# Filler products, a shorter last ranking, an earlier selection matrix and a moved eviction between a delta-rule attention and a sorted mixture of experts

## The chip, the cores and the metric

The kernel runs on one core of a Trainium2 chip. Its time is the device time of one execution in microseconds (us). The core's engines work side by side and wait for each other through semaphores: TensorE (PE, matrix products; its weight loads are listed apart as PEld), VectorE (DVE), ScalarE (ACT), GpSimd (POOL) and SyncE (SP), which here only issues DMA transfers. The profile also shows the share of its full clock that TensorE was granted.

## The reference

An attention block with the delta rule runs over q, k, v of shape (4, 8, 768, 48); its output is read as 3072 tokens of 384 numbers and goes through a mixture of 16 experts (4 groups of 4) of hidden width 1024.

```python
k_n = k / (norm(k) + 1e-6)
for t in range(S):
    y[:, :, t] = q_t @ state
    state = state + beta_t * outer(k_t, v_t - k_t @ state)

x = y.transpose(0, 2, 1, 3).reshape(3072, 384)
g_idx = argmax(x @ w_group);  g_w = softmax(x @ w_group)[g_idx]
e_idx = argmax(x @ w_expert[g_idx]);  e_w = softmax(...)[e_idx]
out = g_w * e_w * (relu(x @ w1[g_idx, e_idx]) @ w2[g_idx, e_idx])
```

Every token goes to one expert.

## The kernel before

**Attention.** The sequence is cut into 24 chunks of 32 steps; one chunk of all four batches fills 128 partitions. Per group of four chunks, `inverse` (L269) inverts the triangular systems on VectorE. The loop over chunks `u` (L675) then does, per chunk: `advance` (L406), whose four steps make a_ps, w_ps, the state update s_bd and the output o_ps, copied to x by ScalarE (L468); and `logits` (L478) for the chunk before, which transposes x (t_ps L485), copies it (xt L489) and multiplies it with the router's weights (l_ps L493, copied to lg L495). x is written to `x_dram` by SP (L733).

**Routing.** `route(r)` (L498) works on a group of chunks: four chunks, and two in each of the last two groups (`groups`, L472). VectorE finds the best group and expert (L516 to L530, `hots` is one-hot), adds up the counts (`acc`, L532), TensorE multiplies with triangular and all-one matrices to rank each token inside its expert (r_ps, L540 and L541), ScalarE copies the ranks (rk, L544) and takes Exp (L545), VectorE makes the rank of each token (`place`, L573), its gate (`what`, third column, L575), the products of `hots` and `what` (`mine`, L577: token's output row, token's input row and gate, for 16 experts) and a one-hot of the place (`at`, L586). TensorE then multiplies `mine` with `at` into s_ps (L593), which ends as a table: for each expert the tokens sent to it. The last group has all of this on the path, since nothing is left to do beside it.

**The order.** In this part it is written by hand: every engine's queue holds its instructions in the order in which the program issues them. `route` and `inverse` are generators; `start` puts them in the list `behind`, `work(n)` lets them issue VectorE work by their share, and `allow(what)` releases those that stopped at a named place (PE_STEP before r_ps, ACT_STEP before the copy of the ranks, SORT before s_ps). After the loop, `while behind` (L736) drains them.

**Handover.** After the loop: n_ps (L745) counts the tokens per expert; `by_place` (L131) turns expert 0's part of s_ps into from_i, to_i and gate; found, last, key, table (L748 to L759) sort the experts by their load. The attention's pools are then closed and those of the experts opened in the same memory. POOL makes a selection matrix `sel` (L926), and gathers the tokens of the first expert from `x_dram` by indirect DMA (`take`, xg, L807), in two tiles of 128 and 96 rows; TensorE transposes them (`turn_in`, t_ps L816), VectorE copies them to xt (L818).

**Experts.** The loop over experts `e` (L951): `hidden` (L846) multiplies xt with w1 in four pairs of column blocks (h_ps L852, 48 records for the 24 products), each pair evicted with Relu by ScalarE (L855); `second` (L865) multiplies with w2 in three thirds of 128 output columns (y_ps L871, two PSUM buffers that take turns), each evicted by ScalarE (yt L873) and followed by `between(j)`, here `late` (L972). At the start of `hidden`, `part_out` (L900) transposes the results of the expert before on VectorE (yq L904), sends them through `y_dram` and reads them back as yr (SP, L908 to L913). `late(0)` transposes the next expert's tokens on VectorE (`cross_in`, xt L832). `late(1)` weighs the results of the expert before with its gates (yo L918, two tiles) and scatters them to the output (POOL, L880). `fetch(e + 2)` issues the gathers of quarter rows for two experts ahead (POOL, xq L824), and after `second` SP issues the weights of expert e + 2 (L164, L171). From expert 1 on the tokens are gathered in quarters, through `quarters` (L836), which uses `sel` (q_ps L841). The last two experts' results leave through TensorE transposes (`turn_out`, L889).

PSUM in the attention part is full: four banks for the state and s_ps, one with tag "s", two with tag "g", one with tag "o" (o_ps).

Of the kernel before, what the change touches and what calls it, by code (L numbers as in the profile page):

```python
# [8 lines left out]
F32 = mybir.dt.float32  # L9
I32 = mybir.dt.int32  # L10
AX = mybir.AxisListType
ALU = mybir.AluOpType
ACT = mybir.ActivationFunctionType
# [53 lines left out]
def deltanet_then_moe(  # L67
# [13 lines left out]
    nc = tc.nc  # L81
# [42 lines left out]
    place = cp.tile([128, NCH], F32, name="place")  # L124
    what = cp.tile([128, NCH, 3], F32, name="what")
    found = cp.tile([128, T, 3, NE], F32, name="found")
    from_i = cp.tile([128, NE, T], I32, name="from_i")
# [47 lines left out]
    with ExitStack() as first:  # L175
# [322 lines left out]
        def route(r):  # L498
# [44 lines left out]
            rk = small("rk", [NE])  # L543
            nc.scalar.activation(rk, r_ps, ACT.Copy)  # L544
            nc.scalar.activation(sx, sx, ACT.Exp)  # L545
# [14 lines left out]
            else:  # L560
                nc.vector.tensor_tensor(rk, rk, hotf, op=ALU.mult)
                yield
# [12 lines left out]
            nc.vector.reciprocal(what[:, u0:u0 + n, 2:3], cw)  # L575
            yield
            (nc.gpsimd if early else nc.vector).tensor_tensor(  # L577
                mine, hotf[:, :, None, :].to_broadcast(like),
                what[:, u0:u0 + n, :, None].to_broadcast(like), op=ALU.mult)
            if early:  # L580
# [57 lines left out]
        with tc.manual_schedule(engines={mybir.EngineType.PE, mybir.EngineType.DVE,  # L638
# [17 lines left out]
            nc.gpsimd.memset(acc[:, 0], 0.0)  # L656
            nc.gpsimd.tensor_copy(what[:, :, 0:2], cut["ids"].rearrange("p (u c) -> p u c", c=2))
            ahead = advance(0)
            next(ahead)
# [13 lines left out]
            allow(FACTOR)  # L673
            ahead_of = {u: [u + LEAD] if u + LEAD < NCH else [] for u in range(NCH + 1)}
            for u in range(NCH + 1):  # L675
                step = advance(u) if u < NCH else iter([None] * 4)
                turned = logits(u - 1) if u else iter([None] * 2)
# [56 lines left out]
                if pieces and u + LEAD >= NCH:  # L734
                    pieces.pop(0)()
            while behind:  # L736
                work(2)
                allow(PE_STEP)
                allow(ACT_STEP)
                allow(SOON)  # L740
                allow(NEXT)
                allow(SORT)

            n_ps = ps.tile([128, NE], F32, tag="s", name="n_ps")
            nc.tensor.matmul(n_ps, lhsT=ones, rhs=acc[:, NCH], start=True, stop=True)  # L745
            by_place(s_sort.rearrange("p (t c e) -> p t c e", t=T, c=3)[:, :, :, 0:FIXED],
                     slice(0, FIXED))
# [116 lines left out]

    def second(hid, yt, w2, between):  # L865

        R = hid.shape[2]
        for j in range(DC):
            y_ps = ps.tile([128, R], F32, tag="y", name="y_ps")
            for f in range(FC):  # L870
                nc.tensor.matmul(y_ps, lhsT=w2[:, f, j * 128:(j + 1) * 128], rhs=hid[:, f],  # L871
                                 start=(f == 0), stop=(f == FC - 1))
            nc.scalar.activation(yt[:, j, 0:R], y_ps, ACT.Copy)  # L873
            between(j)
        return yt
# [45 lines left out]
    def turned():  # L921
        return mp.tile([128, DC, T * TILE], F32, tag="xt", name="xt")

    ready = {e: take(from_i[:, e], tiles_of[e]) for e in range(FIXED)}
    sel = mp.tile([128, 4, 4, BL], F32, name="sel", bufs=1)
    nc.gpsimd.tensor_copy(sel, ident.rearrange("p (g r) -> p g r", r=BL)[:, :, None, :].to_broadcast(  # L926
        [128, 4, 4, BL]))
    xts, yts, rows_of, evs = {0: turned()}, {}, {}, {}
# [15 lines left out]
    with tc.manual_schedule(engines={mybir.EngineType.PE, mybir.EngineType.DVE, mybir.EngineType.SP,  # L944
# [6 lines left out]
        for e in range(NE):  # L951
# [33 lines left out]
            hid = hidden(xts.pop(e), SLOTS[e], w1, early)  # L985
            second(hid, yts[e], w2, late)
            if e + 2 < NE:
# [100 lines left out]
```

## Time and profile before

| what | us |
|---|---|
| median of 4 runs (517.68 to 519.12) | 518.31 |
| the profiled execution's own time | 519.45 |
| its span, first to last instruction | 517.5 |
| TensorE busy, share of the span | 471.2 (91%) |
| attention, with its start, up to the last o_ps | 228.6 |
| last o_ps to the first h_ps (handover) | 15.8 |
| first h_ps to the last product of the last expert | about 264 |
| from there to the span's end | about 9 |

The span is what the profile shows; about 1.95 us of the execution lie outside of it. A page has one digit for each of 40 slices of 12.9 us: busy tenths of each engine and, under PEclk, the clock that TensorE was granted. The chain of waits is followed back from the last instruction: at each place it names what ended the wait. A matmul of fp32 operands is listed as two records. Ends of matmuls are modelled, so a record shows somewhat more than the time its columns take.

### The profile page before, as it was taken

The page shows a single profiled execution, that of the slowest core. Times are in us where ns is not written, and L with a number is a line of the kernel's source. Part 1 is how long each engine was busy: PE and PEld are TensorE (multiplying, and loading weights), DVE is VectorE, ACT ScalarE, POOL GpSimd, SP SyncE. Part 2 cuts the span into 40 slices and gives each one's busy share as a digit, 9 for nine tenths or more (in the row PEclk, how much of TensorE's full clock was granted, in tenths as well). Part 3 has the DMA queues.
Part 4 walks back from the last instruction along what each step waited for, and adds up shares of the span by engine and source line. Part 5 has one row for each costly group of instructions (what it writes and reads, how often), then busy time and mean ns, then how long its engine had stood idle before and what let it go on. Part 6 is the DMA issues. An engine that isn't in the chain of part 4 may idle for free.

```text
span 517.5 us, 18175 instructions
## 1 busy us (share of the span) xinstructions
PE 471.2 (91%) x7814; PEld 436.6 (84%) x7814; DVE 246.6 (48%) x815; ACT 190.6 (37%) x404; POOL 193.5 (37%) x288
## 2 busy tenths in 40 slices
PE   3447999999999999984999999999999999999993
PEld 3335878888888888873999999999999999999992
DVE  3999999999999994335420111011101111101110
ACT  3224777677776767640111111211111111111210
POOL 0040300624608243002265544564445644365131
PEclk9999999999999999995899999999999999999998
DMA  5681445444323545100878687878878988788820
GB/s 175 234 288 66 152 146 169 155 146 142 140 87 113 164 157 175 42 33 27 245 254 270 209 280 228 259 250 290 258 233 274 324 289 266 255 255 282 302 71 20
DMA packets 57330, 99.93 MB, mean 193 GB/s; under 512 B 18973, under 2 KB 41431, under 8 KB 57249
## 3 DMA queue, kind: packets, MB, share of 16 engines
q1 hardware_dynamic: 51329, 88.76, 52.3%
q0 software_dynamic: 5920, 10.00, 6.3%
q8 instruction: 62, 1.02, 0.8%
q14 instruction: 19, 0.16, 0.1%
HBM read 84.61 MB, written 14.27 MB: 191 GB/s over the span
## 4 chain that ended last, share of the span: by engine, by line
PE 69%; DMA 9%; DVE 6%; issue 5%; POOL 5%; ACT 4%; SPq 0%; POOLq 0%; DVEq 0%; ACTq 0%
PE h_ps L852 19%; PE y_ps L871 18%; DMA out_dram<-yo,to_i 6%; PE w_ps L435 5%; PE s_ps L445 5%; PE a_ps L418 3%; PE l_ps L493 3%; ACT s_bd L451 3%; POOL xq L824 3%; PE o_ps L459 3%; PE o_ps L427 3%; PE g_ps L247 2%; PE a_ps L412 2%; PE t_ps L485 2%; PE s_ps L593 2%
## 5 line engine op out<-in xcount | busy, mean ns | idle before, releaser
L852 PE MATMUL h_ps<-xt,w 128*128 128x224 f32 (+15 forms) x768 | 135.0, 337 | 0.6 <-DVE xt L818 0.6
L852 PEld LDWEIGHTS h_ps<-xt,w 128*128 128x128 f32 x768 | 131.5, 193 | 1.7 <-DVE xt L818 0.8
L871 PE MATMUL y_ps<-hid,w 128*128 128x224 f32 (+15 forms) x768 | 132.2, 332 | 0.0
L871 PEld LDWEIGHTS y_ps<-hid,w 128*128 128x128 f32 x768 | 129.1, 190 | 0.3
L824 POOL DMA_INDIRECT xq<-x_dram,from_q x92 | 87.6, 953 | 40.6 <-issue 23.8
L918 DVE TENSOR_SCALAR yo<-yr,gate 128x384 f32<-128x384 f32 (+14 forms) x28 | 11.5, 418 | 168.6 <-DMA yr<-y_dram 156.1
L855 ACT ACTIVATE hid<-h_ps 128x448 f32<-128x448 f32 (+15 forms) x64 | 32.1, 501 | 114.2 <-PE h_ps L852 114.2
L880 POOL DMA_INDIRECT out_dram<-yo,to_i x32 | 34.1, 1064 | 76.5 <-DVE yo L918 61.7
L873 ACT ACTIVATE yt<-y_ps 128x224 f32<-128x224 f32 (+15 forms) x48 | 16.1, 336 | 111.9 <-PE y_ps L871 111.9
L356 DVE TENSOR_TENSOR t<-m 128x81 f32<-128x81 f32 (+13 forms) x156 | 52.0, 333 | 0.2
L362 DVE TENSOR_TENSOR m<-m,t 128x81 f32<-128x81 f32 (+13 forms) x156 | 51.7, 332 | 0.0
L451 ACT ACTIVATE s_bd<-s_ps 48x768 f32<-48x768 f32 x46 | 37.0, 804 | 13.1 <-PE s_ps L445 12.5
L339 DVE SCALAR_TENSOR_TENSOR m<-m 128x29 f32<-128x29 f32 (+27 forms) x174 | 40.7, 237 | 0.4
L384 ACT ACTIVATE mtb<-mt,con 128x256 f32<-128x256 f32 x47 | 34.4, 744 | 0.0
L247 PE MATMUL g_ps<-kqt 48*32 48x64 f32 (+1 forms) x1216 | 18.7, 241 | 15.5 <-issue 9.3
L435 PE MATMUL w_ps<-f,mtb 64*64 64x48 f32 x768 | 28.0, 224 | 1.7 <-DVE mtb L382 1.7
L247 PEld LDWEIGHTS g_ps<-kqt 48*32 48x32 f32 x1216 | 14.6, 118 | 17.7 <-issue 11.7
L418 PEld LDWEIGHTS a_ps<-s_bd,kqt 128*32 128x32 f32 x736 | 15.4, 111 | 15.5 <-ACT s_bd L451 7.3
L435 PEld LDWEIGHTS w_ps<-f,mtb 64*64 64x64 f32 x768 | 25.1, 138 | 3.9 <-ACT mtb L384 1.9
L532 POOL TENSOR_TENSOR acc<-acc,hots 128x16 f32<-128x16 f32 x16 | 5.3, 330 | 60.1 <-DVE hots L530 59.1
L445 PE MATMUL s_ps<-w,kv 32*128 32x96 f32 x736 | 27.3, 286 | 0.0
L904 DVE STREAM_TRANSPOSE yq<-yt 128x672 f32<-128x672 f32 (+2 forms) x14 | 11.9, 852 | 29.1 <-ACT yt L873 29.1
(142 smaller groups left out, 563.3 us busy)
## 6 DMA issues: line engine op xcount, KB each, us to landing
w<-in_w_dram SPq DMA_DIRECT2D x29, 1536.0 KB, 8.4
kv<-in_kv_dram SPq DMA_DIRECT2D x24, 448.0 KB, 3.2
kqt<-in_kq_dram SPq DMA_DIRECT2D x20, 512.0 KB, 3.9
x_dram<-x SPq DMA_DIRECT2D x24, 192.0 KB, 2.0
w<-in_w_dram SPq DMA_DIRECT2D x24, 128.0 KB, 3.4
y_dram<-yq SPq DMA_DIRECT2D x36, 84.0 KB
yr<-y_dram SPq DMA_DIRECT2D x14, 192.0 KB, 2.5
kqt<-in_kq_dram SPq DMA_DIRECT2D x8, 256.0 KB, 3.4
```

The costliest lines, as they stand in the source:

```text
L247: nc.tensor.matmul(g_out[quads[b], hh * NP + j, of], lhsT=kqt[rows, 0, j, quads[b]], rhs=kqt[rows, of, j, quads[b]], start=True, stop=True ...
L339: nc.vector.scalar_tensor_tensor(row, in0=m[:, j, 0:j], scalar=m[:, i, j:j + 1], in1=row, op0=ALU.mult, op1=ALU.add)
L356: nc.vector.tensor_tensor(tv, m[:, j + 2:, j:j + 1].to_broadcast([128, n, j]), m[:, j:j + 1, 0:j].to_broadcast([128, n, j]), op=ALU.mult)
L362: nc.vector.tensor_tensor(below, below, tv, op=ALU.add)
L384: nc.scalar.activation(mtb[:, rows, a], from_, ACT.Copy, scale=by)
L435: nc.tensor.matmul(w_ps[b, h], lhsT=mt[b, uu * H + (h % 2) * NP + h // 2], rhs=f[b, h], start=True, stop=True, skip_group_check=True)
L445: nc.tensor.matmul(s_at[:, b, j], lhsT=k[quads[b], j], rhs=w[quads[b], 2 * j:2 * j + 2], start=(u == 0 and j == 0), stop=True, skip_group_ ...
L451: nc.scalar.activation(s_bd[rows, :, :, hh, :], s_at[rows, :, :, hh * D:(hh + 1) * D], ACT.Copy)
L824: nc.gpsimd.indirect_dma_start(out=xq[:, g, :], out_offset=None, in_=x_dram[:, :].rearrange("n (q c) -> (n q) c", q=4), in_offset=bass.Ind ...
L852: nc.tensor.matmul(h_ps[:, k], lhsT=w1[:, j, (f + k) * 128:(f + k + 1) * 128], rhs=xt[:, j, 0:R], start=(j == 0), stop=(j == DC - 1), skip ...
L871: nc.tensor.matmul(y_ps, lhsT=w2[:, f, j * 128:(j + 1) * 128], rhs=hid[:, f], start=(f == 0), stop=(f == FC - 1))
L880: put = nc.gpsimd.indirect_dma_start(out=out[:, :], out_offset=bass.IndirectOffsetOnAxis(ap=to[0:P, i:i + 1], axis=0), in_=yo[0:P, :], in_ ...
```

## The change

It has five parts.

- `idle_products` multiplies the identity with the first n columns of the constant `below` into a tile i_ps that nobody reads, in the bank with tag "o". It is called with 192 columns at the start of the pass after the last chunk; with 384 and 192 after the loop; again with 384 and 192 when the last group's r_ps has been issued; and four times 384 after n_ps.
- In the last group the ranks are not copied by ScalarE: VectorE multiplies r_ps with `hots` straight from its bank. The first two of the three parts of `mine` are made ahead of that, the third where all three were.
- In the drain after the loop, `allow(PE_STEP)` is called once, when a task waits there.
- `sel` is made by POOL in the prologue, in the constants' pool, instead of after the handover.
- For experts 1 to 14 the middle third of y is evicted by VectorE instead of ScalarE. VectorE's queue has it behind the transpose of the next expert's tokens and ahead of the two weighings yo.

```diff
+    sel = cp.tile([128, 4, 4, BL], F32, name="sel")
...
-            nc.scalar.activation(rk, r_ps, ACT.Copy)
+            final = r == len(groups) - 1
+            if not final:
+                nc.scalar.activation(rk, r_ps, ACT.Copy)
...
-                nc.vector.tensor_tensor(rk, rk, hotf, op=ALU.mult)
+                if final:
+                    nc.vector.tensor_tensor(
+                        mine[:, :, 0:2], hotf[:, :, None, :].to_broadcast([128, n, 2, NE]),
+                        what[:, u0:u0 + n, 0:2, None].to_broadcast([128, n, 2, NE]), op=ALU.mult)
+                nc.vector.tensor_tensor(rk, r_ps if final else rk, hotf, op=ALU.mult)
...
+            cs = slice(2 if not early and final else 0, 3)
+            like[2] = cs.stop - cs.start
             (nc.gpsimd if early else nc.vector).tensor_tensor(
-                mine, hotf[:, :, None, :].to_broadcast(like),
-                what[:, u0:u0 + n, :, None].to_broadcast(like), op=ALU.mult)
+                mine[:, :, cs], hotf[:, :, None, :].to_broadcast(like),
+                what[:, u0:u0 + n, cs, None].to_broadcast(like), op=ALU.mult)
...
             nc.gpsimd.tensor_copy(what[:, :, 0:2], cut["ids"].rearrange("p (u c) -> p u c", c=2))
+            nc.gpsimd.tensor_copy(sel, ident.rearrange("p (g r) -> p g r", r=BL)[:, :, None, :]
+                                  .to_broadcast([128, 4, 4, BL]))
...
+            def idle_products(*columns):
+
+                i_ps = ps.tile([128, H * D], F32, tag="o", name="i_ps")
+                for n in columns:
+                    nc.tensor.matmul(i_ps[:, 0:n], lhsT=ident, rhs=cut["below"][:, 0:n], start=True,
+                                     stop=True, skip_group_check=True)
+
             for u in range(NCH + 1):
+                if u == NCH:
+                    idle_products(H * D // 2)
...
+            idle_products(H * D, H * D // 2)
+            ranked = False
             while behind:
                 work(2)
-                allow(PE_STEP)
+                if not ranked and PE_STEP in held.values():
+                    ranked = True
+                    allow(PE_STEP)
+                    idle_products(H * D, H * D // 2)
...
             nc.tensor.matmul(n_ps, lhsT=ones, rhs=acc[:, NCH], start=True, stop=True)
+            idle_products(*[H * D] * 4)
...
-    def second(hid, yt, w2, between):
+    def second(hid, yt, w2, between, by_vector=()):
...
-            nc.scalar.activation(yt[:, j, 0:R], y_ps, ACT.Copy)
+            if j in by_vector:
+                nc.vector.tensor_copy(yt[:, j, 0:R], y_ps)
+            else:
+                nc.scalar.activation(yt[:, j, 0:R], y_ps, ACT.Copy)
             between(j)
...
-    sel = mp.tile([128, 4, 4, BL], F32, name="sel", bufs=1)
-    nc.gpsimd.tensor_copy(sel, ident.rearrange("p (g r) -> p g r", r=BL)[:, :, None, :].to_broadcast(
-        [128, 4, 4, BL]))
...
-            second(hid, yts[e], w2, late)
+            second(hid, yts[e], w2, late, (1,) if 0 < e < NE - 1 else ())
```

H * D is 384 here. Of an idle product's values nothing is used.

## The prediction

> **What bounds the kernel now.** I read the page first, then busy time by stretches, then the chain of waits around the handover from attention to experts, then the instructions in order of time there.
>
> ```profile
> PE 471.2 (91%) x7814; PEld 436.6 (84%) x7814; DVE 246.6 (48%) x815; ACT 190.6 (37%) x404; POOL 193.5 (37%) x288
> ...
> PEclk9999999999999999995899999999999999999998
> ```
>
> TensorE is busy 91% of the span, and its clock falls once in the middle, in slices 19 and 20 (233 to 259 us). The stretches, with columns time, PE, PEld, DVE, ACT, POOL busy (instructions), granted clock, DMA share, GB/s:
>
> ```profile
> 226.49:229.91 3.42, 2.81 (x83) 2.62 (x82) 1.79 (x10) 1.20 (x6) 0.00 (x0) 1.00 0.02 5
> 229.91:233.32 3.41, 1.96 (x16) 1.72 (x15) 1.60 (x9) 0.60 (x2) 0.00 (x0) 1.00 0.16 58
> ...
> 233.00:233.50 0.50, 0.50 (x4) 0.43 (x4) 0.32 (x3) 0.00 (x0) 0.00 (x0) 0.82 0.00 0
> ...
> 243.56:246.97 3.41, 2.86 (x9) 2.35 (x8) 2.98 (x6) 0.00 (x0) 0.00 (x0) 0.50 0.00 0
> ...
> 250.00:250.50 0.50, 0.50 (x3) 0.46 (x3) 0.43 (x3) 0.00 (x0) 0.20 (x2) 0.61 1.00 246
> ...
> 270.00:500.00 230.00, 230.00 (x1378) 229.50 (x1377) 32.81 (x56) 43.25 (x101) 113.03 (x127) 1.00 0.81 260
> ...
> 513.00:513.50 0.50, 0.00 (x0) 0.00 (x0) 0.00 (x0) 0.00 (x0) 0.00 (x0) 0.71 0.00 0
> ```
>
> From 270 us on PE is never idle: what moves the first expert moves the end. The mixed slices date the clock's changes: down at 233.32, up at 250.39, down again at 513.21 in the tail. The distances 17.07 and 262.82 stand as 5 to 77, so both are multiples of 3.413 us: the clock is judged on a grid of that step. The stretch before the fall had PE busy 1.96 of 3.41 us (58%), the one before it 82% and did not fall; 84% at half clock (243.56) did not raise it, a full one did. So "down" lies between 58 and 82% by this measure, "up" over 84%. Where the grid lies against the program is not set by the kernel.
>
> The chain of waits (start, length, what):
>
> ```profile
> 228.64 0.50 ACT x L468
> ...
> 229.18 0.56 PE t_ps L485 x3
> ...
> 232.88 0.41 PE r_ps L540 x2
> ...
> 233.66 0.21 ACT rk L544
> ...
> 235.62 1.96 PE s_ps L593 x8
> ...
> 238.60 1.34 POOL xg L807
> ...
> 240.25 2.81 DMA xg<-x_dram,from_i
> ...
> 243.11 0.76 PE t_ps L816 x3
> ```
>
> Every engine waits for the next one here, and each PE piece runs at half clock from 233.32 on. Two lines of the instructions in order show the selection copy ahead of the gather, and the first expert:
>
> ```profile
> 237.77 0.61 POOL L926 COPY sel<-con 128x512 f32<-128x512 f32 x1 [34.86 <-DVE from_i L133]
> ...
> 244.40 12.28 PE L852 MATMUL h_ps<-xt,w 128*128 128x224 f32 x48 [0.55 <-DVE xt L818]
> ```
>
> The same expert's second product, as many matmuls of 224 columns at full clock, takes 3.11 + 3.03 + 3.05 = 9.19 us in the chain. So 3.1 us are lost to the clock, half of the 5.99 us from 244.40 to 250.39.
>
> **The change part by part.** One column of a full-clock record costs 9.19 us / 48 / 224 = 0.855 ns; a product of 384 columns is two records, 0.66 us, one of 192 is 0.33.
>
> 1. Idle product ahead of t_ps. It shares its bank with o_ps, so it waits for the copy x (end 229.14), as t_ps did: it stands after the pause, on the chain. +0.33 (0 if it hides in t_ps's start, +0.66 at half clock).
>
> 2. Products of 576 columns after the last l_ps: 0.99 us in the pause 231.68 to 232.88, which hides them with 0.2 to spare. At half clock the cover is gone: r_ps about 0.8 later. The next 576, after r_ps, lie in the pause 233.56 to 235.62: hidden at either speed, but for about 0.3.
>
> 3. Ranks from their bank. r_ps at full clock is 0.26 + 0.23 (the group at 210.77) for 0.70: -0.21. From its end to rk on DVE were 0.31 through ScalarE; reading the bank leaves about 0.04 (s_ps to from_i had 0.02). But two thirds of mine now stand ahead of rk on DVE: about 0.2 (rows from 128x32, 0.19, to 128x96, 0.26) after sx's end at 233.35, so rk starts at 233.55 where it started at 233.89: -0.34 in all (ends -0.48 and 0, if reading the bank is dear). What ACT loses was waited for, and Exp goes up one place. mine's last third: 0.26 to 0.19, -0.07.
>
> 4. s_ps: 1.96 at half clock, 0.99 for eight such records at 215.98: -0.97 (0 if the clock is low).
>
> 5. sel off POOL's queue. The gather started 1.02 us after s_ps's end (237.58 to 238.60). The waits that stood at sel now stand at the gather; for the next expert it started 0.28 after from_i's end (248.80 to 249.08), so 0.02 + 0.16 + 0.30 = 0.48 after s_ps: -0.54 (ends -0.2 and -0.9: its own 1.34 against 0.95 of the others). SP's queue is untouched. In the prologue sel passes all of POOL's attention work: after `what` (29.09 + 0.24) 0.61 us, with POOL's next work at 32.10. It delays only DVE, which is full there: L339 took 0.30 to 0.34 with POOL at work, 0.23 without; two or three instructions, +0.1 (0 to 0.6).
>
> 6. Four products of 384 after n_ps: 2.63 us, done about 2.8 after s_ps's end. The first gathered tile was there at 242.01, 3.41 after the gather's start, so now 0.48 + 3.41 = 3.9 after s_ps: hidden with 1.1 to spare. At half clock they need 5.3 and hold t_ps 1.8 us.
>
> 7. t_ps of the second tile at full clock: 0.76 to about 0.5 (0.33 back to back at 260.60): -0.26.
>
> 8. h_ps of the first expert: 12.28 to 9.2: -3.08 (ends: 0 and -3.08).
>
> 9. Middle third of y by VectorE for experts 1 to 14. PE waits for neither copy. On DVE the two yo now queue behind it. For expert 2 they ran at 297.49 and 298.23, ACT's copy of that third at 300.98 (0.35): yo moves to about 301.4, its scatters from 298.18 to about 302.1 and 303.4, done at 304.5. POOL's next work came at 305.34, DVE's next transpose at 304.40, and the gathers behind feed an expert that starts over 10 us later. SP's w loads wait for none of it. Near the end yo is late anyway (481.51, waiting for yr). Zero, bounds 0 to +0.5.
>
> Sum: to s_ps's end +0.33 - 0.34 - 0.07 - 0.97 = -1.05; to h_ps's start -0.54 - 0.26 more = -1.85; with h_ps -4.93; prologue +0.1: -4.83. Against the profiled execution's own 519.45: 514.6. Its 517.5 span has 1.95 around it, unchanged. It stands 1.14 over the median of the runs (518.31, 517.68 to 519.12). I put that down mostly to the grid: from h_ps's start to the rise can be 3.41 to 6.83 us, a loss of 1.7 to 3.4, and the profile lost 3.1. If the clock holds, that luck goes, so I keep 514.6 for the median too.
>
> [...] The trace's fall at 233.32 came with no PE pause over 1.19 us behind it. [...]
>
> **The rivals.**
>
> *The clock falls once more, after the products.* From their end (2.8 after s_ps) to h_ps's start (6.0 after: 244.40 - 1.85 against 237.58 - 1.05) lie 3.2 us with two t_ps of about 0.55: a grid step laid over it has PE busy 1.1 + 0.2 of 3.41, 40%, under the 58% that fell. By the 58% mark some 1.5 of 3.4 us of grid positions do so, 44%; by 82% nearly all. Against it: the 58% were thin (20 and 48 columns), these are full-width streams; by columns streamed, at 0.855 ns, the step that fell had about 11% (6 of 20, 4 of 48, 4 of 32 columns), this one would have 24% (672 columns and the products' last 0.26). Which measure the chip uses the trace does not say. Price: 3.41 us at half clock, +1.7, in a third of these positions +3.2: 516.3 to 517.8.
>
> *The clock isn't held at all* (products too few): items 4, 7 and 8 stay as before, and 1, 3, 5 leave -0.4 to -0.6, offset by the delay of item 2: against the median 517.8.
>
> *Slower: the clock falls ahead of the products.* The step 228.6 to 232.0 would hold PE for 76%. If the mark of the fall is over 76%, all runs at half clock from 232 on: to s_ps's end +0.33 (item 1) + 0.83 (the 576 end late) + 0.1 (r_ps) - 0.41 (item 3) + 0.3 (the 576 behind r_ps hold s_ps) = +1.15, 238.7. n_ps and the four products end 0.35 + 5.3 later, 244.4; two t_ps (0.88, 0.75) and the copy (0.55) follow: h_ps starts at 246.5, +2.1. With h_ps at half clock as before that is 520.4 against the median. What decides is whether the products' own busy stretch holds a whole grid step: where it does, h_ps is fast and the sum is near 518.
>
> **How the numbers follow.** Clock held in most runs 0.56: 514.6, its own range 513.8 (item 5 at -0.9, item 3 at -0.48) to 515.6 (items 5, prologue and 9 at their dear ends). Falls after the products in most runs 0.27: 516.3 to 517.8. Not held 0.07: 517.8. Slower rival 0.10: half at 518, half at 520.4. The range 513.8 to 517.8 holds the first two and part of the third. 0.3% is 1.55 us, about what a measurement here can tell from no change: faster is below 516.76. Faster: 0.56 and over half of 0.27, 0.72; within: 0.19; slower: 0.09.
>
> **What would show it.** Right: clock 1.00 from 226 to 513; s_ps x8 near 1.0; i_ps ended before the first t_ps; the gather 0.5 after s_ps; h_ps x48 near 9.2; PE 100% busy after. Wrong: 0.50 in any step near 242 and h_ps over 10.5; r_ps waiting for i_ps; PE idle between experts with y_ps waiting for DVE; sel stretching DVE's work at 29 us.

## The result: a third of the gain that was forecast

| | before | after |
|---|---|---|
| median, us | 519.15 (70 runs, 517.02 to 523.24) | 517.54 (44 runs, 514.64 to 523.26) |
| profiled execution's own time, us | 519.45 | 517.78 |
| its span, us | 517.5 | 516.0 |

The ratio of after to before is 0.9968, with a 95% interval of 0.9955 to 0.9981: a gain of 1.66 us on 519.15, where 4.83 were forecast. The direction was right, and 514.6 us was wrong by 2.9.

The page of the changed kernel, busy time and the clock in 40 slices:

```profile
PE 473.7 (92%) x7832; PEld 437.4 (85%) x7832; DVE 250.9 (49%) x830; ACT 185.9 (36%) x389; POOL 194.2 (38%) x288
...
PEclk9999999999999999999899999999999999999998
```

Where before had a 5 in the twentieth slice (half clock for 17 us), after has an 8: the clock is not lost at 233 us, but it is lost once. The stretches of the changed kernel, cut on the clock's own grid (columns: time, PE, PEld, DVE, ACT and POOL busy, granted clock, DMA share, GB/s):

```profile
231.28:234.69 3.41, 3.00 (x21) 2.32 (x19) 1.69 (x10) 0.52 (x2) 0.00 (x0) 1.00 0.06 19
...
238.10:241.52 3.42, 2.40 (x8) 1.12 (x6) 1.55 (x6) 0.00 (x0) 2.15 (x2) 1.00 0.19 54
241.52:244.93 3.41, 1.75 (x10) 1.36 (x11) 1.77 (x4) 0.00 (x0) 0.00 (x0) 1.00 0.15 47
244.93:248.34 3.41, 3.41 (x11) 3.05 (x10) 3.37 (x3) 0.00 (x0) 0.00 (x0) 0.50 0.30 96
...
270.00:500.00 230.00, 230.00 (x1381) 229.54 (x1380) 35.25 (x68) 38.59 (x87) 109.53 (x123) 1.00 0.79 256
```

The products carry the clock to 241.52. The step behind them, with the two t_ps and two pauses in it, has PE busy for 1.75 of 3.41 us, and the next one, in which the first expert begins, runs at half clock. From 270 us on PE is never idle, as before. The chain of waits over the handover (start, length, what):

```profile
230.10 0.59 PE i_ps L690 x2
230.69 0.34 PE t_ps L486 x3
...
234.17 0.41 PE r_ps L541 x2
...
234.84 0.19 DVE rk L568
...
236.54 1.11 PE s_ps L602 x8
...
238.82 1.20 POOL xg L833
...
243.15 0.48 PE t_ps L842 x3
...
244.17 11.03 PE h_ps L878 x48
```

The ranks go from TensorE's bank to VectorE without ScalarE between, s_ps takes 1.11 instead of 1.96, t_ps 0.48 instead of 0.76, and h_ps 11.03 instead of 12.28 (at full clock it takes 9.35, as experiments below show). POOL's row shows what did not come:

```profile
238.82 1.20 POOL L833 DMA_INDIRECT xg<-x_dram,from_i  x1 [35.00 <-DVE key L779]
```

The selection copy is gone from ahead of the gather, and yet the gather starts 1.17 us after s_ps's end (237.65). With the copy it was 1.02.

The two profiled executions, stage by stage:

| stage | before | after | change | forecast |
|---|---|---|---|---|
| start to the last o_ps's end | 228.57 | 229.49 | +0.92 | +0.1 |
| to s_ps's end | 8.99 | 8.14 | -0.85 | -1.05 |
| to the first h_ps | 6.84 | 6.54 | -0.30 | -0.80 |
| first expert's h_ps | 12.28 | 11.03 | -1.25 | -3.08 |
| to the span's end | 260.84 | 260.83 | -0.01 | 0 |
| outside the span | 1.93 | 1.75 | -0.18 | 0 |
| sum | 519.45 | 517.78 | -1.67 | -4.83 |

Over half of what is missing is in h_ps. The executions say the same with their granted clock. The record lists it for 46 of them, the profiled one included; two of them, at 522.46 and 523.26 us, lie over 1.5% above the fastest and are left out here. Of the other 44, 12 were granted 0.994 or more over the whole span, with a mean of 516.25 us; 14 were granted 0.991 to 0.993, as the profiled one with its single lost step, with a mean of 517.49; 16 were granted 0.980 to 0.990, with means of 519.1 and 519.9 for their upper and lower part. The last two stand at 0.978 and yet at 515.52 and 517.18 us, so a lost step does not cost time everywhere. By this mean, the clock was held in about a quarter of the runs and not in most of them, and where it was held the time still stood 1.65 over the forecast.

### The profile page after: what moved, and what is told of

It is laid out like the page before. It is cut to its first block, busy times and chain, and to the rows that moved or that the text cites. A ratio compares the mean times of both kernels' runs of the same rounds, so it can differ in the third digit from the quotient of the medians.

```text
span 516.0 us, 18196 instructions
## 1 busy us (share of the span) xinstructions
PE 473.7 (92%) x7832; PEld 437.4 (85%) x7832; DVE 250.9 (49%) x830; ACT 185.9 (36%) x389; POOL 194.2 (38%) x288
## 3 DMA queue, kind: packets, MB, share of 16 engines
q8 instruction: 63, 1.03, 0.8%
## 4 chain that ended last, share of the span: by engine, by line
PE 56%; issue 12%; DMA 11%; POOL 9%; DVE 6%; ACT 4%; SPq 0%; POOLq 0%; ACTq 0%; DVEq 0%
PE h_ps L878 12%; PE y_ps L897 12%; DMA out_dram<-yo,to_i 9%; POOL xq L850 6%; PE w_ps L436 5%; PE s_ps L446 5%; PE a_ps L419 3%; PE l_ps L494 3%; ACT s_bd L452 3%; PE o_ps L460 3%; PE o_ps L428 3%; PE g_ps L248 2%; PE a_ps L413 2%; PE t_ps L486 2%; PE s_ps L602 2%
## 5 line engine op out<-in xcount | busy, mean ns | idle before, releaser
L900 DVE COPY yt<-y_ps 128x232 f32<-128x232 f32 (+13 forms) x14 | 5.1, 366 | 133.4 <-PE y_ps L897 133.4
L902 ACT ACTIVATE yt<-y_ps 128x224 f32<-128x224 f32 (+15 forms) x34 | 11.4, 336 | 116.6 <-PE y_ps L897 116.6
```

## The experiments

Two theories stood after the result. One: the clock fell in the step behind the products because that step was too empty, and the loss goes when it is filled. Its rival: the products do not hold the clock, and what after gains comes from the shorter chain. Beside this, three things were open: why the gather did not move, whether the moved eviction costs anything, and what, beside busy time, tells the steps that lose the clock.

### The products left out

```diff
 def idle_products(*columns):
+    return
...
     for n in columns:
```

> The changed kernel with all idle products left out (the ranks from their bank, sel in the prologue and the eviction by VectorE stay). If the products are what the change gained by: the clock falls near 233 us or one grid step later, s_ps x8 takes about 1.96, the first h_ps 10.9 to 12.6, and the time against before is 0.3 to 0.5 us lower at most (ratio 0.999 to 1.000, against 0.9968 of the changed kernel). If the gain came from the ranks and sel instead: ratio near 0.997 all the same.

520.75 us against 521.82 of the kernel before, timed beside it, ratio 0.9986 (0.9967 to 1.0005). In its trace the clock is half from 234.75 to 251.82, 17.07 us as before, s_ps takes 1.96 and h_ps 12.20. Without the products the other four parts are worth about 0.7 us, within what this can tell from nothing. The prediction had -0.4 to -0.6 for this case.

### The gap behind the products filled

```diff
-            idle_products(*[H * D] * 4)
+            idle_products(*[H * D] * 6, 256)
...
             turn_in(ready[0], xts[0], i, tiles_of[0][i], "to"[i])
+        i_ps = ps.tile([128, 192], F32, tag="y", name="i_ps")
+        nc.tensor.matmul(i_ps, lhsT=ident, rhs=cut["below"][:, 0:192], start=True, stop=True)
```

> The changed kernel with six products of 384 and one of 256 after n_ps instead of four of 384, and one of 192 behind the second t_ps. If the clock falls because the stretch between the products' end and h_ps's start is thin: no fall in the middle in nearly any run (mean granted clock 0.993 or more), the first h_ps 9.2, the time about 1.3 us under the changed kernel's middle (ratio 0.994 to 0.995). If it falls for another reason: granted clocks spread as in the changed kernel (0.978 to 0.995) and the ratio stays at 0.997, or above it if the products hold t_ps back.

518.34 us, ratio 0.9916 (0.9885 to 0.9947). PE in order of time in this kernel (start, busy, what, shape, idle before):

```profile
238.53 4.55 PE L690 MATMUL i_ps<-con 128*128 128x384 f32 x14
...
244.02 0.47 PE L842 MATMUL t_ps<-con,xg 96*128 96x96 f32 x3 [0.29 <-DMA xg<-x_dram,from_i]
244.33 0.52 PE L975 MATMUL i_ps<-con 128*128 128x192 f32 x2
245.04 9.35 PE L878 MATMUL h_ps<-xt,w 128*128 128x224 f32 x48 [0.20 <-DVE xt L844]
```

The clock stays at 1.00 from 54.5 us to the tail, and h_ps takes 9.35 us in the chain. In the trace the first theory holds: the step behind the products was what lost the clock, and filling it keeps it; four of its six runs were granted 0.995 or more. The ratio does not show the gain by itself: the next two kernels, timed beside this one with the gap left open, come out as low. This trace and those of the kernels without products, without the first product and with a gather used before show one more thing, which the traces of before, of after and of the five kernels from the moved eviction to the thin products do not: PE waits for y_ps in the expert stage, 0.37 us in all here, up to 1.5. The kernel before, timed beside these four, stood at 521.82, so the ratios count and not the times.

### The first product left out

```diff
             for u in range(NCH + 1):
-                if u == NCH:
-                    idle_products(H * D // 2)
```

> The changed kernel without the 192 columns ahead of the last t_ps. If that product only stands in the way: from the copy x to t_ps 0.04 instead of 0.6, the chain 0.34 shorter, ratio 0.996. If it holds the clock in the first grid steps: more runs with granted clocks under 0.99, and a ratio of 0.997 to 0.999.

518.6 us, ratio 0.992 (0.9892 to 0.9948). t_ps starts 0.04 us after x instead of 0.63 after it and takes 0.56 instead of 0.34: the product costs 0.37 us on the chain. The trace has the clock at half from 244.26 to 247.67 and h_ps at 11.03, as after. The saving of 0.37 us does not explain a ratio 0.005 under after's own; after itself was not timed beside it, so how much of that is the product stays open.

### A gather that had been used before

```diff
+    zero_i = cp.tile([32, 1], I32, name="zero_i")
+    early_rows = cp.tile([32, DM], F32, name="early_rows")
...
+            if u == NCH: nc.gpsimd.indirect_dma_start(out=early_rows[:, :], out_offset=None,
+                in_=w2_d.rearrange("e f d -> (e f) d"), in_offset=...(ap=zero_i[:, 0:1], axis=0))
```

> The changed kernel with a small indirect gather of 32 rows from w2 issued on POOL at the start of the pass after the last chunk; its rows are not used. If the first gather of the tokens starts about 0.9 after its wait is over because it is the first of its kind: it now starts 0.3 to 0.4 after, and takes 0.95 instead of 1.2; the first h_ps starts 0.6 to 0.8 earlier, ratio 0.9955. If VectorE's work or the waits ahead of it hold it: the start stays 0.85 to 1.0 after from_i's end and the ratio at 0.997.

517.22 us, ratio 0.9915 (0.9885 to 0.9945). The gather takes 1.03 instead of 1.20 us, but it starts 0.89 us after from_i's end, 1.00 in after: that POOL had not gathered before is not why it starts late. The profiled execution, 522.19 us, was one of two of the ten with a clock of 0.98, and it shows the prediction's slower rival alive (the chain of waits):

```profile
235.91 1.28 PE i_ps L693 x3
...
237.88 2.08 PE i_ps L693 x4
239.96 1.57 PE s_ps L604 x8
...
241.91 4.21 PE i_ps L693 x8
...
247.83 9.35 PE h_ps L885 x48
```

Here the clock fell at 231.18, ahead of the products. Then the products are no longer hidden: they stand on the chain at half speed, and h_ps starts 17.6 us after the last o_ps, where it was 15.83 before. Their own stretch brings the clock back at 244.84, so h_ps is fast.

### The moved eviction alone

The kernel before, with only this:

```diff
-            nc.scalar.activation(yt[:, j, 0:R], y_ps, ACT.Copy)
+            (nc.vector.tensor_copy(yt[:, j, 0:R], y_ps) if j in by_vector else
+             nc.scalar.activation(yt[:, j, 0:R], y_ps, ACT.Copy))
```

> The kernel before with one part of the change alone: for experts 1 to 14 the middle third of y is copied by VectorE instead of ScalarE. The theory (item 9) prices it at 0: no PE idle between the first expert and the tail, and from the end of the first h_ps to the span's end 260.8 us as in the traces of before and after. The rival, from the small PE pauses that the four runs so far show in the expert stage (y_ps starting 0.4 to 1.7 us late in all, 261.5 to 263.1 us to the span's end): the moved copy makes ScalarE late for its next one; then this trace has such pauses and the kernel is 1 to 2 us slower than the kernel before (ratio 1.002 to 1.004).

519.53 us against 519.08, ratio 1.0006 (0.9984 to 1.0028). No PE wait stands between 260 and 500 us in its trace, and from the end of the first h_ps to the span's end it takes 260.83 us, as before and after. So the moved eviction by itself does not make y_ps late. What did in the first four kernels stays open: no trace of the kernel before was taken beside them.

### The selection copy put back

The changed kernel, with the copy into `sel` behind the line that gathers the first expert's tokens, as before.

> The changed kernel with the selection matrix made where it stood before, on POOL's queue ahead of the first gather. If the gather's start hung on sel (item 5), it goes back from s_ps's end + 1.17 us to about s_ps's end + 1.6 or more. The rival: a gather starts 0.87 us after the separate waits ahead of it, and sel ran inside that time; then the gather stays at s_ps's end + 1.0 to 1.2, and all that sel's place changes is the prologue, where the VectorE instruction at 30 us goes back from 0.58 to about 0.23 us.

One execution, 519.94 us. POOL in order of time (start, length, what, idle before and its releaser):

```profile
238.51 0.61 POOL L952 COPY sel<-con 128x512 f32<-128x512 f32 x1 [35.32 <-PE n_ps L767]
239.34 1.34 POOL L830 DMA_INDIRECT xg<-x_dram,from_i  x1 [0.22 <-DVE key L776]
```

s_ps ended at 238.32: the gather starts 1.02 us later, exactly as in the kernel before, and 0.15 earlier than without the copy. The copy cost the gather nothing. In this execution h_ps took 12.27 us: behind the products the clock was lost for two steps (244.10 to 250.93), the dearer case of the rival. In the prologue, VectorE's instruction at 30 us is back at 0.23; in after, with the copy beside it, VectorE has this row:

```profile
30.44 0.58 DVE L340 SCALAR_TENSOR_TENSOR m<-m 128x22 f32<-128x22 f32 x1
```

That is not the price of the copy's place. In the nine other traces with the copy in the prologue this instruction takes 0.23 too, and the copy 0.60 to 0.73 where it took 0.94 in after: in after the two happened to meet.

### The gather's waits taken earlier

```diff
+    xg_first = cp.tile([128, T, DM], F32, name="xg_first")
...
+            nc.gpsimd.indirect_dma_start(out=early_rows[:, :], out_offset=None, in_=x_dram[:, :],
+                in_offset=bass.IndirectOffsetOnAxis(ap=zero_i[:, 0:1], axis=0))
             n_ps = ps.tile([128, NE], F32, tag="s", name="n_ps")
...
-    ready = {e: take(from_i[:, e], tiles_of[e]) for e in range(FIXED)}
+    ready = {e: take(from_i[:, e], tiles_of[e], xg_first) for e in range(FIXED)}
```

> The changed kernel with the first expert's gathered rows in a tile of their own that nothing had used, and one gather of 32 rows of x, put on POOL's queue ahead of n_ps, which takes up the waits for the stores of x some 5 us earlier. The first expert's gather then waits itself for from_i and for nothing else. Theory (the separate waits cost the gather 0.87 us): it starts about 0.3 us after from_i's end as the next expert's does, s_ps's end + 0.45 to 0.5 instead of + 1.17, and takes 1.03 to 1.1 instead of 1.20; the first t_ps comes 0.7 to 0.85 us earlier, the PE pause ahead of it is 1.1 instead of 1.9 us, and the time falls by about 0.8 against the changed kernel, more where the shorter pause keeps the clock. Rival (a gather that follows DVE's write of its list needs 0.9 to 1.0 us whatever it waits on): the start stays at + 1.0 to 1.2 and nothing is gained.

516.03 us, ratio 0.9954 (0.993 to 0.9978). In the changed kernel five separate instructions on POOL's queue wait for the stores of x, for from_i and for the memory that the tile takes over; only then comes the gather. Here the gather waits for from_i itself, with the separate waits done before. POOL's row:

```profile
237.46 0.99 POOL L841 DMA_INDIRECT xg_first<-x_dram,from_i  x1 [3.71 <-DVE from_i L137]
```

It starts 0.49 us after s_ps's end (236.97), 0.29 after from_i's (237.17), and takes 0.99. That settles item 5: in after the gather behind separate waits started 0.87 us after the last of them (237.955 to 238.823; 0.88 for the added early gather of this kernel), and in the kernel before the selection copy ran inside this time: its gather started 0.91 us after the last wait (237.692) with the copy in between. A rival would be that POOL had stood idle for 35 us in after and for 3.7 here. This kernel's next gather speaks against it: it comes 8.2 us after another one, has separate waits ahead of it, and starts 0.71 us after the last (247.464 to 248.178). The first t_ps starts 3.65 us after s_ps's end, where it was 4.81 in after, and the chain of waits now goes by the second tile:

```profile
238.75 3.03 DMA xg_first<-x_dram,from_i
...
241.83 0.48 PE t_ps L850 x3
...
242.84 9.35 PE h_ps L886 x48
```

h_ps starts 5.87 us after s_ps's end (after: 6.54), and in this execution the clock held. Five of its twelve runs had a clock of 0.994 or more (mean 515.1), the others 0.967 to 0.992: a shorter pause alone does not hold the clock in every run.

### The pauses closed

```diff
-                    idle_products(H * D // 2)
+                    nc.tensor.matmul(s_ps[:, 3, 0:256], lhsT=ident, rhs=cut["below"][:, 0:256], ...)
...
-                    idle_products(H * D, H * D // 2)      # behind r_ps
+                    idle_products(H * D, H * D)
...
-            idle_products(*[H * D] * 4)
+            idle_products(*[H * D] * 5)
...
+        i_ps = ps.tile([128, 192], F32, tag="y", name="i_ps")
+        nc.tensor.matmul(i_ps, lhsT=ident, rhs=cut["below"][:, 0:192], start=True, stop=True)
```

This is the kernel of the early waits with four edits to the products.

> The kernel of the early waits, with the pauses closed further: the first product is 256 columns in a free bank of the state, so that it runs while ScalarE makes x and not after it; the second product behind r_ps is 384 columns instead of 192; five products of 384 follow n_ps instead of four; and one of 192 follows the second t_ps. Theory (the clock falls in any grid step that PE's pauses leave too empty, before or behind the products): the clock stays at 1.00 through the handover in nearly all runs, the first h_ps takes 9.2 to 9.35 us, the product of 256 costs nothing on the chain, and the ratio to the kernel before is 0.988 to 0.991. Rival (what is left of the fall comes ahead of the products, in the step around 228 to 232 us, whatever is put there): half clock from about 231 us in some runs, their time 4 us over the others', ratio 0.992 or more.

515.2 us against 519.08, ratio 0.9912 (0.9885 to 0.9939). In the handover its trace has the clock at 1.00 and h_ps at 9.35. The first product, in a free bank, starts where o_ps ends, at 231.52 (PE in order of time; ends are modelled, so that records overlap a little):

```profile
231.45 0.70 PE L699 MATMUL s_ps<-con 128*128 128x256 f32 x2
232.13 0.55 PE L489 MATMUL t_ps<-con,x 128*128 128x128 f32 x3
```

No pause is left between o_ps and t_ps; t_ps ends 1.16 us after o_ps's end, where it was 1.53 in after. It is not the clock's last fall: this execution (517.44, the slowest of six) lost the step 75.71 to 79.12, in the attention.

### The same products, thin

```diff
-    nc.tensor.matmul(i_ps[:, 0:n], lhsT=ident, rhs=cut["below"][:, 0:n], ...)
+    nc.tensor.matmul(i_ps[0:32, 0:n], lhsT=ident[0:32, 0:32], rhs=cut["below"][0:32, 0:n], ...)
```

and so for the first product and the one behind t_ps.

> The kernel of the closed pauses with every idle product of the handover made from a corner of 32 rows by 32 columns of the identity instead of 128 by 128: as many columns stream and TensorE is busy as long at full clock, but a sixteenth of the array works. Theory (in all ten traces so far the clock falls only after a grid step in which the array did under about 0.32 of what it could, counting each record's columns by the rows and the width it uses; busy time does not separate them): these products count for almost nothing, the clock falls at about 3 to 7 us after the last o_ps in every run, the products then take twice as long and stand in the way, s_ps x8 takes about 1.96 us, the five products behind n_ps about 6.6 us, the first h_ps starts about 20 us after the last o_ps (before: 15.83) and most of it runs at half clock, the granted clock is 0.96 to 0.98, and the ratio to the kernel before is 1.004 to 1.010. Rival (busy time, or columns streamed, decides): nothing differs from the kernel of the closed pauses, clock 0.99 or more in most runs, ratio 0.989 to 0.993.

522.45 us against 518.85, ratio 1.0062 (1.0046 to 1.0078). PE in order of time:

```profile
235.82 2.12 PE L694 MATMUL i_ps<-con 32*32 32x384 f32 x4
...
243.80 6.60 PE L694 MATMUL i_ps<-con 32*32 32x384 f32 x10
...
252.57 1.86 PE L889 MATMUL h_ps<-xt,w 128*128 128x224 f32 x4
```

h_ps starts 19.86 us after the last o_ps (232.71); its row ends here at the edge of the window. The stretches of the same kernel, with the columns as above:

```profile
232.21:235.62 3.41, 2.95 (x67) 2.35 (x55) 1.40 (x9) 1.17 (x3) 0.00 (x0) 1.00 0.18 62
235.62:239.04 3.42, 3.42 (x11) 1.73 (x11) 1.89 (x11) 0.24 (x1) 1.10 (x1) 0.50 0.05 14
239.04:242.45 3.41, 3.41 (x9) 1.24 (x7) 1.63 (x10) 0.00 (x0) 0.00 (x0) 0.50 0.00 0
242.45:245.86 3.41, 3.41 (x11) 1.97 (x12) 2.06 (x9) 0.00 (x0) 1.57 (x2) 0.50 0.06 14
245.86:249.28 3.42, 3.42 (x7) 0.90 (x6) 0.00 (x0) 0.00 (x0) 0.35 (x1) 0.50 0.27 87
```

TensorE is busy without a pause for four steps on end, the products stream as many columns in all as the full ones, and the clock neither holds nor comes back until the first expert's own products (256.10). So here neither busy time nor columns kept the clock. What sets these products apart from the full ones is how much of the array works: by the count of the next section four of these steps have a share of 0.03 to 0.08, where the three steps of after with full products in them (231.28 to 241.52) have 0.41 to 0.69. (Both the rows and the width were cut, so which of the two counts this run does not say.) One part of the theory's forecast missed: not most of h_ps but its first 3.5 us ran at half clock.

### The prologue filled too

```diff
                 gram(u, homes[u % len(homes)])
+                i_ps = ps.tile([128, H * D], F32, tag="s", name="i_ps")
+                for n in ((H * D, H * D, H * D // 2) if u < LEAD - 1 else (H * D,) * 3):
+                    nc.tensor.matmul(i_ps[:, 0:n], lhsT=ident, rhs=cut["below"][:, 0:n], ...)
```

> The kernel of the closed pauses, with full-width products of 384, 384, 192 and three times 384 columns also in TensorE's two pauses of the prologue (34.1 to 37.6 and 38.6 to 43.0 us in the trace of the closed pauses). Until about 53 to 55 us every kernel so far runs TensorE at half speed (a pair of products that takes 0.87 us later takes 1.65 at 50 us) and TensorE is busy without a pause from 46.4 us on. Theory (the clock rises after a grid step in which the array works through, and holds where it does over about 0.32 of what it could): the clock is up by 45 us or earlier, w_ps, s_ps, o_ps and a_ps of the first steps take 1.1, 1.1, 1.1 and 0.9 instead of 1.95, 2.04, 1.95 and 1.65 us, the last o_ps ends 2 to 4.5 us earlier, at 226 to 229 us, and the ratio to the kernel before is 0.982 to 0.988. Rival (the front is bound by VectorE's inverse, not by TensorE): the first steps are faster but TensorE then waits, the last o_ps ends where it did (229 to 231.5 us), and the ratio stays at 0.990 to 0.993.

514.26 us against 518.85, ratio 0.992 (0.9897 to 0.9943). TensorE in order of time at the first steps, in the kernel with the closed pauses alone:

```profile
46.80 2.04 PE L449 MATMUL s_ps<-w,kv 32*128 32x96 f32 x32
48.76 1.95 PE L463 MATMUL o_ps<-w,gqm 64*64 64x48 f32 x32
50.63 1.65 PE L416 MATMUL a_ps<-vh,con 128*128 128x384 f32 x2
```

And with the prologue filled:

```profile
44.99 1.15 PE L449 MATMUL s_ps<-w,kv 32*128 32x96 f32 x32
46.07 1.13 PE L463 MATMUL o_ps<-w,gqm 64*64 64x48 f32 x32
47.13 0.91 PE L416 MATMUL a_ps<-vh,con 128*128 128x384 f32 x2
...
71.65 1.14 PE L463 MATMUL o_ps<-w,gqm 64*64 64x48 f32 x32 [1.49 <-DVE gqm L268]
72.71 1.36 PE L416 MATMUL a_ps<-vh,con 128*128 128x384 f32 x2
```

The clock is up at 38.90 instead of 55.23, and the first steps run at full speed, as the theory said. But at 70 us TensorE then waits 1.49 us for VectorE's second inverse; the step of that wait loses the clock again (73.04 to 76.45), and the last o_ps ends at 228.49, no earlier than in the traces of before (228.57) or of the early waits (228.83), though 3.0 us earlier than in that of the closed pauses (231.52), which lost a step in the attention. That end lies in the theory's range, the ratio in the rival's: the waits at VectorE's inverse and the step lost with it take back at least part of what TensorE wins in front.

### That pause filled as well

```diff
                 if not ahead_of[u]:
                     next(step)
+                if u == 3:
+                    i_ps = ps.tile([128, H * D], F32, tag="s", name="i_ps")
+                    for n in (H * D, H * D // 2): nc.tensor.matmul(i_ps[:, 0:n], ...)
                 next(step)
```

> The kernel with full-width products in the prologue too, and two more (384 and 192 columns, 0.99 us) in TensorE's pause of 1.49 us at 70.15 us, ahead of the o_ps that waits for VectorE's second inverse. In the kernel without them the grid step from 69.62 us had the array at 0.16 of what it could, and the step after it ran at half clock. Theory (the clock falls after a step under about 0.32): these products bring that step to about 0.45, the clock is held from about 39 us to the tail, a_ps and o_ps behind the pause take 0.91, 0.87 and 0.85 instead of 1.36, 1.51 and 1.40 us, the last o_ps ends 1.0 to 1.7 us earlier than without (228.5), near 227, and the ratio to the kernel before is 0.986 to 0.990. Rival (what is won there is waited for again at the next inverse, or the clock falls for another reason): the last o_ps ends at 228 to 230 us and the ratio stays at 0.990 to 0.993.

514.31 us against 518.62, ratio 0.9902 (0.9881 to 0.9923). The step around 72 us now holds, and a_ps and o_ps behind it take 0.91, 0.87 and 0.84 us as forecast. But in the profiled execution the prologue's products ended 1.68 us too soon for w_ps, that step fell (45.34 to 52.17 at half clock), and the last o_ps ends at 228.45 again where 227 was forecast. The intervals of the last three full-width kernels overlap: what the prologue adds to the closed pauses cannot be told from nothing. Each of them beats the kernel before, by 0.8 to 1.0%, and its whole interval lies under after's.

## The clock in these traces, counted

With thirteen traces it can be counted which steps lost the clock. For every grid step of 3.413 us at full clock, from the clock's first rise to the last product, I added up the records' columns, each multiplied by the rows and the width of the array that its shape names (128\*128, 32\*32 and so on) over 128 times 128, by the 0.855 ns of a full-clock column in before's trace, and divided by 3413 ns: the share of the array's work in that step. It is worked out from the records, of which some are missing, so it is a little rough.

| share of the array in a step | steps at full clock | of these, followed by half clock |
|---|---|---|
| under 0.20 | 4 | 4 |
| 0.20 to 0.26 | 9 | 5 |
| 0.26 to 0.325 | 16 | 4 |
| 0.325 to 0.40 | 151 | 0 |
| over 0.40 | 1519 | 0 |

All 13 falls lie under 0.325, none of 1670 steps above it fell. (The fall in the tail, behind the step in which the products end, is not counted.) Of the steps that held, 15 lie at or under the highest share that fell; counted by rows alone it would be 173 steps, by width alone 497, by columns alone 1187, so neither alone separates the steps as their product does. PE's busy share in the 13 runs from 0.36 to 1.00. The one at 1.00 is this, in the trace with the selection copy put back:

```profile
216.79:220.21 3.42, 3.42 (x59) 3.26 (x62) 1.11 (x5) 1.48 (x4) 0.00 (x0) 1.00 0.02 5
220.21:223.62 3.41, 3.41 (x97) 3.12 (x94) 1.75 (x8) 1.67 (x3) 0.00 (x0) 0.50 0.00 0
```

Its share was 0.29: the attention's small products (32\*32, 64\*64) took all of the time and little of the array. Of 36 steps at half clock, all 11 with a share of 0.417 or more (0.5 is the most there) were followed by full clock, and 2 of the 25 below. Between 0.20 and 0.325 9 of 25 steps fell and 16 did not, so in that band the count does not tell them apart.

The changes of the clock stand on a grid of 3.413 us: the stretches at half clock around the handover took 3.41 us in after, 6.83 with the selection copy put back, 13.66 with the gather used before, 17.07 in before and without the products, 20.48 with the thin ones, which is 1, 2, 4, 5 and 6 steps. Where the grid lies differs between executions: after and the kernel with the gap filled are the same program up to n_ps, and their clocks first rise at 53.79 and at 54.5 us. Busy time does not tell which steps fall: the one at 216.79 above had TensorE busy throughout and lost the clock, and with thin products four busy steps did not bring it back. What the chip itself judges by was not shown.

## Why the prediction was wrong

**Item 8 failed**, h_ps 12.28 to 9.2, -3.08. It measured 11.03, -1.25, and the step of the working that failed is the rival's rebuttal. The rival (the clock falls once more, after the products) was described as it came: the step over the two t_ps, one grid step at half clock, 516.3 to 517.8 us; it came at 1.68 us (11.03 against 9.35) and 517.54. It was given 0.27 because that step would have 24% of the columns where the step that fell in before had 11%. The 24% was compared with the one step that fell and not with those that held. In before's trace the thinnest full-clock step that held has a share of 0.58 by columns streamed (216.25) and of 0.27 by the array (226.49): 24% lies under everything that had been seen to hold. By busy time, the prediction's other measure, the step of after had 51%, under the 58% that fell; the column count was what talked this down. The comparison would have taken the safety away, not foretold the fall: the step of after that fell had an array share of 0.32, more than the 0.27 that held in before, in the band where some fall and some hold. Nor does the prediction's mark by busy time, a fall between 58 and 82%, stand: steps at 80 to 100% fell in later traces. That 517.54 lies inside the range of 513.8 to 517.8 is owed to this rival, which the range took in, and not to the sum.

**Item 5 failed.** The gather's start moved by +0.15 where -0.54 was forecast, 0.69 late; the stage was 0.50 over, since the gather itself took 1.20 and not 1.34. The 0.28 of the next expert's gather was the price of a gather that waits by itself on one semaphore. The prediction said that sel's waits would stand at the gather; that the gather behind separate waits would start only 0.87 us after them, as it did in after, it did not see, since sel's 0.61 us ran inside that time. With the waits taken early the forecast's 0.48 came out as 0.49.

**Prologue.** +0.35 at VectorE's instruction in after's trace where +0.1 was taken, inside its ends of 0 and 0.6, and none at that instruction in nine others. The last o_ps ended +0.92 later in after, but over all the traces it ends between 228.4 and 232.7, and three of those with the copy in the prologue, two of them with filler there, end at 228.45 to 228.83, beside 228.57 before. So the copy's part in the 0.92 is not shown; the spread between executions is larger.

**What held.** Item 1: +0.37 from x to t_ps's end (+0.33 forecast). Item 2: the products hidden, with a pause of 0.15 left ahead of r_ps (0.2). Item 3: r_ps's start to s_ps's start 2.74 to 2.37, -0.37 (-0.41). Item 4: -0.85 (-0.97). Item 6: done 2.86 us after s_ps's end (2.8), and PE then waited. Item 7: -0.28 (-0.26). Item 9: 0, on its own and in the sum. What the slower rival describes was seen too: in one trace, of the kernel with a gather used before, the clock fell at 231.18, ahead of the products.

**Against the profiled 517.78,** 3.16 over the forecast: h_ps 1.83 (1.68 for the clock and 0.15 since it takes 9.35 at full clock and not 9.2), the front 0.82, the stretch from s_ps to h_ps 0.50, that to s_ps 0.20, less 0.18 outside the span.

## What to carry to other kernels

Before filling pauses to keep TensorE's clock, look at every grid step that is left, the one behind the filler too: in after that one lost the clock, with PE busy for 1.75 of 3.41 us. Count the array's work beside busy time: in these traces PE was busy for between 0.36 and 1.00 of the time in the 13 steps that fell, and all 13 had the array under a share of 0.325, where 16 others held. Trust a step only where it lies over everything that was seen to fall. With the gap filled and with the pauses closed, full-width filler held the clock through the profiled handover (h_ps 9.35 us); thin filler did not, and the half clock lasted 20.48 us. When something is taken off a queue ahead of a critical instruction, ask what that instruction's own start-up did meanwhile: here the waits moved to the gather, which started 1.17 us after s_ps's end without the copy and 1.02 with it. Filler is safe only where it is hidden at half speed as well: in one trace the clock fell ahead of it, and h_ps started 17.6 us after the last o_ps, where it was 15.83 before.

## What the runs showed of the hardware

- With the selection copy put back, a step of 3.413 us with TensorE busy all through and an array share of 0.29 lost the clock (216.79 to 220.21); with thin products four such busy steps with shares of 0.03 to 0.08 did not bring it back (235.62 to 249.28).
- A gather on POOL started 0.27 to 0.29 us after the write that it waited for itself, and 0.71 to 0.88 us after the last of separate wait instructions ahead of it; it took 1.20 us in after, 1.03 where another gather had run before, and 0.99 with its waits taken early.
- In one execution VectorE's 0.23 us instruction took 0.58 while POOL copied 128x512 beside it, and POOL's copy 0.94 instead of 0.61.
- Until its first rise, at 52 to 55 us without filler in the prologue, the clock is not on record, and TensorE took nearly twice as long: a_ps of two records took 1.65 us at 50.63 with the pauses closed, and 0.91 with the prologue filled, where the clock was up at 38.90.
